# Splitting a single row maximum into two half products in a gated mix of two attentions

## The chip, the cores and the metric

The kernel runs on one core of one Trainium2 chip. The metric is the device time of one execution in microseconds; for the kernel before it was measured in three runs. Engines are named as in the profile: PE is TensorE's matmul, PEld its weight load, DVE is VectorE, ACT is ScalarE, POOL is GpSimd and SP is the queue that issues most DMAs.

## What is computed

The input x has 2048 rows of 512. Two attentions with 32 heads of 16 columns each are computed on it, and a gate per row mixes them. Branch A looks back at 8 keys in steps of two rows. Branch B lets all 32 query heads share one key head and one value head, over all 2048 keys. Everything is float32. The change touches branch B only.

```python
def _B_ref(x, wq, wk, wv, wo):
    q = (x @ wq).reshape(B, S, H, Dh).transpose(0, 2, 1, 3)
    k = x @ wk
    v = x @ wv
    scores = jnp.einsum("bhqd,bkd->bhqk", q, k) * (Dh ** -0.5)
    p = _softmax(scores, axis=-1)
    o = jnp.einsum("bhqk,bkd->bhqd", p, v)
    return o.transpose(0, 2, 1, 3).reshape(B, S, H * Dh) @ wo
...
x = A_x
g = _sigmoid((x * gate_w).sum(-1, keepdims=True))
return g * _A_ref(x, A_wqkv, A_wo) + (1 - g) * _B_ref(x, B_wq, B_wk, B_wv, B_wo)
```

## The kernel before

**Stages.** A front part (up to about 280 us) projects keys, values and queries. Then follows a loop of 512 steps plus one, in which branch B's attention runs on PE, ACT and DVE, while POOL works through branch A and DMAs move data between the two. Two output phases interrupt the loop; they multiply finished rows by the output weights. The last rows' output products are spread over the loop's last steps.

**Units and steps.** A unit is four heads and 512 queries; there are 32 units (`NU`). A step takes 128 keys for one unit, so a unit has 16 steps. The scores of a step are computed with keys on the partitions and queries along the free axis. `exp_pair` (line 570, its products at line 576) makes the *first scores*, two heads into the pair of banks pe0, and later in the step the *second scores*, the other two heads into pe1. Of the two heads, one uses array rows 0 to 63 and the other rows 64 to 127 (`odd`), so their two products can run side by side. Behind each, ACT takes one exponential of both banks (128x1024, line 578) into a tile `pexp`. Each bank pair exists once: the next step's first scores can be loaded only when the exponential that reads pe0 has ended, and so with pe1. At the end of a step `weighted` (line 586) multiplies the *previous* step's four `pexp` halves by the values, into the bank po; these products use all 128 rows of the array.

**Maxima ahead.** The exponentials need each query's largest score. It is computed for a later unit while the present one is in its steps, from products of its own: 128 queries against 512 keys, one head at a time (`max_mm`, line 395). A *pair* (`fill_pair`, line 425) computes both heads into the two banks of `pm` and VectorE reduces them in one instruction (line 433). A *single* (`fill_one`, line 437) computes one head into the bank `ps` (called `m1` in the code), which VectorE reduces at line 445. The results go to the unit's tile `mx`, one column per chunk of 512 keys; when all are there, `filled` reduces the columns (line 413), and a few small operations put the maxima into the query tile of the unit as extra rows. In output phases, sums and differences of keys (line 483) yield the maxima of two chunks at once.

**What sets the order.** The program is written out by a planner as it runs: `clk` holds its estimate of each engine's time, `free` when a bank will be free, and `T_...` its prices. A step's order is `(0, "m2", "later")`: first scores, a pair if its banks will be free, then the second scores with a single ahead of them or behind. `singles(s)` decides whether the step gets a single, from a running share and from how far DVE lags. `bare` remembers that the last step had none. The single goes ahead of the second scores if their banks are not expected to be free yet:

```python
if which == "later":
    order[:0] = ["m1", 1] if free["e1"] > clk["pe"] - E1S or bare[0] and free["m1"] < clk["pe"] - 1.0 else [1, "m1"]
    first = 0
```

A step without a single is called *plain* here, one with a single a *single step*. In the order of this kernel 209 steps are plain and 269 have a single, of which 60 have it behind the second scores; 34 further steps hold output products or end the loop. Plain and single steps mostly alternate. Every engine works through its instructions in the order of the program.

Of the kernel before, what the change touches and what calls it, by code (L numbers as in the profile page):

```python
# [6 lines left out]
F32 = mybir.dt.float32  # L7
F32R = mybir.dt.float32r
AF = mybir.ActivationFunctionType
ALU = mybir.AluOpType  # L10
AX = mybir.AxisListType
PSUM = bass.MemoryType.PSUM

P = 128
# [3 lines left out]
DH = 16  # L18
# [6 lines left out]
NU = NQB * NHG  # L25
# [10 lines left out]
NB = 10  # L36
# [14 lines left out]
LAG = 6  # L51


T_F, T_R, T_LAT, T_EXP, T_RED2, T_RED1, T_W, T_TTR = 0.235, 0.23, 0.20, 0.92, 1.14, 0.61, 1.21, 0.70


# [32 lines left out]
def gated_mix_kernel(ctx, tc, xt, wa, wk, wq, wo_a, wo_b, out):  # L89
    nc = tc.nc  # L90
# [42 lines left out]
    def after(eng, ready, dur):  # L133
        clk[eng] = max(clk[eng], ready) + dur
        return clk[eng]
# [91 lines left out]
    nc.vector.tensor_reduce(mk[:, 5:6], ident.rearrange("p (y s t) -> p y s t", s=2, t=8)[:, :, 1, :], AX.XY, ALU.add)  # L227
    nc.vector.tensor_scalar(mk[:, 4:5], mk[:, 5:6], -2.0, 1.0, op0=ALU.mult, op1=ALU.add)
    nc.vector.memset(mk[:, 6:7], -FMAX)
    whole_k = cp.tile([P, 2, DH], F32, name="wholek")  # L230
    halves_of = cp.tile([P, 2, P], F32R, name="sel")
    nc.vector.tensor_add(whole_k, twin[:, :, 0, :, 0], twin[:, :, 0, :, 1])
    for x in range(2):
# [139 lines left out]
    slots = [(0, 0, t, 2 * g + kc) for g in range(2) for t in range(2) for kc in range(2)]  # L373
    slots += [(0, pr, t, kc) for pr in range(2) for t in range(4) for kc in range(4) if pr or t > 1]
    slots += [(v, pr, t, kc) for v in range(1, NU) for pr in range(2) for t in range(4) for kc in range(4)]
    half = []
    free = {"m2": 0.0, "m1": 0.0, "e0": 0.0, "e1": 0.0, "po": 0.0}
    tasks, shifted = [], set()
    hooks, pool, done = [], 0.0, set()
# [1 line left out]
    def fillable():  # L381
        return bool(half) or bool(slots) and slots[0][0] < len(stacked) and stacked[slots[0][0]] <= clk["pe"]

    def unit_tile(v):
        for x in (v, v + 1):
            if x < NU and x not in left:
                mx[x] = wp.tile([P, 2, 2, 4, 4], F32, name="mx", bufs=3)
                nc.gpsimd.memset(mx[x], -FMAX)
                charge(250)
                left[x] = NF // NU  # L390
        return mx[v]
# [11 lines left out]
        issued[0] += 1  # L403

    def to_go():
        return 2 * len(slots) + len(half)

    def filled(v, n):
        left[v] -= n
        if not left[v]:  # L410
            ms = wp.tile([P, 2, 2, 8], F32, name="ms")
            m = mx.pop(v).rearrange("p b i t k -> p b (i t) k")
            nc.vector.tensor_reduce(ms, m.unsqueeze(2).to_broadcast([P, 2, 2, 8, 4]), AX.X, ALU.max)
            after("dve", 0, 0.32)
            if pe:
                tasks.append((clk["pe"] + 0.5, maxima_turn, (v, ms)))
            else:
                maxima_turn(v, ms)
# [3 lines left out]
        nc.vector.transpose(mt, ms.rearrange("p b x y -> p (b x y)"))  # L422
        tasks.append((after("dve", 0, 0.34) + (2.0 if formed and not pe else 0.1), shift_a, (v, mt)))

    def fill_pair(dst, key):
        if dst is m2:
            dst = m2.whole()
        v, pr, t, kc = slots.pop(0)
        m = unit_tile(v)
        mark("m20", "m21")  # L430
        for odd in range(2):
            max_mm(dst[:, odd, :], v, pr, t, kc, odd)
        nc.vector.tensor_reduce(m[:, :, pr, t, kc], dst, AX.X, ALU.max)  # L433
        free[key] = after("dve", after("pe", 0, T_R) + T_LAT, T_RED2) + 0.08
        filled(v, 2)

    def fill_one(dst=m1, key="m1"):
        if not half:
            v, pr, t, kc = slots.pop(0)
            half.extend([(v, pr, t, kc, 0), (v, pr, t, kc, 1)])  # L440
        v, pr, t, kc, odd = half.pop(0)
        m = unit_tile(v)
        mark(key)
        max_mm(dst, v, pr, t, kc, odd)
        nc.vector.tensor_reduce(m[:, odd, pr, t, kc:kc + 1], dst, AX.X, ALU.max)  # L445
        free[key] = after("dve", after("pe", 0, T_R) + T_LAT, T_RED1) + 0.08
        filled(v, 1)


    dd, formed, ended, wants = [], {}, set(), []  # L450
# [477 lines left out]
    def spread(js, n):  # L928

        m = 3 * (C + n)  # L930

        parts_a(js[0])
        yield 1.0
        while slots or half or free["m2"] > clk["pe"] + 0.1:
            yield 1.0
        for j in js:
            nxt = j + 1 if j != js[-1] else None
            items = []
            for i in range(m):
                if j == js[0] and i < 3 * C and (j, 1) not in turned:  # L940
                    while i == 3 * C - 3 and NU - 3 not in shaped:
                        yield 1.0
                    if NU - 3 in shaped:
                        prepare(j, n, nc.gpsimd.tensor_copy)
                items = items or out_items(j, n, (0, 1))
                st, mv = items[i]
                for b in range(2):
                    h = slice(64 * b, 64 * b + 64)
                    nc.tensor.matmul(m2[:, b, :], st()[h], mv[h], start=(i == 0), stop=(i == m - 1 and (b == 1 or nxt is not None)))  # L949
                after("pe", 0, T_R)  # L950
                row_prods[0] -= 1
                row_left[0] = m - 1 - i
                if i == 1 and j + 2 <= js[-1]:
                    blocks_both(j + 2)
                if i == 3 * C and nxt:
                    parts_a(nxt)
                if i < m - 1:
                    yield 0.0
            del turned[j, 0], turned[j, 1]
            if nxt:  # L960
                prepare(nxt, n, nc.gpsimd.tensor_copy)
            x = len(parts)
            if x < 2:
                spare.append((p2[0] if x else p2b[0]).tile([P, 512], F32, name="part", tag=("own", "tr8")[x], bufs=1))
            elif x == 2:
                two = p2[0].tile([P, 2, 512], F32, name="part", tag="pr", bufs=1)
                spare.extend([two[:, 0, :], two[:, 1, :]])
            parts[j] = spare[x]
            if nxt:
                nc.vector.tensor_copy(parts[j], m2[:, 1, :])  # L970
                nc.vector.tensor_add(parts[j], m2[:, 0, :], parts[j])
                after("dve", clk["pe"] + T_LAT, 1.4)
                yield 1.5
        done.add("last")
# [22 lines left out]
    def single_share(s):  # L997

        left = 16 * (NU - 1) - 16 - s
        if left > 0:  # L1000
            most = to_go() - 2 * left - PER_ROW * max(0, NJ - 4 - outs) - 2 * (left > 5)
            rate = most / left
            if len(stacked) < NU:
                ready = len(half) + 2 * sum(x[0] < len(stacked) for x in slots[:16 * NB])
                wait = max(1, 16 * (home(len(stacked))[1] + 1) + LAND - s)
                rate = min(rate, ready / wait - 2)
            share[0] = min(2.0, share[0] + max(0.0, min(1.0, rate)))
        else:
            share[0] = 1.0

    share, bare, step = [0.0], [False], [0]

    def fill_ready(key, slack):
        if fillable() and free[key] <= clk["pe"] + slack:
            clk["pe"] = max(clk["pe"], free[key])
            if key == "m1":
                fill_one()
            elif half and (not slots or slots[0][0] >= len(stacked) or stacked[slots[0][0]] > clk["pe"]):
                fill_one(m2[:, 0, :], "m2")
            elif slots:  # L1020
                fill_pair(m2, "m2")

    def pause(most):
        n = 0
        while n < most and slots and fillable():
            key = min(("e0", "e1", "m2"), key=lambda k: free[k])
            clk["pe"] = max(clk["pe"], free[key])
            if half:
                fill_one({"e0": eb[0], "e1": eb[1], "m2": m2}[key][:, 0, :], key)
                n += 1  # L1030
                continue
            fill_pair({"e0": eb[0], "e1": eb[1], "m2": m2}[key], key)
            n += 2
        return n
# [335 lines left out]
    for s in range(NS + 1):  # L1370
# [7 lines left out]
        if s < NS and kt == 0 and u not in shifted:  # L1378
            while u not in shifted:
                clk["pe"] += 0.5  # L1380
                run_tasks()
                if u not in shifted and left.get(u, 1):
                    assert pause(4)
        v = min(x[0][0] for x in (half, slots, [(NU,)]) if x)
        need = left.get(v, NF // NU)
        steps = 16 * v - 6 - s
        short = need - 2.8 * max(0, steps) if v < NU else 0
# [20 lines left out]
        elif short > 0 and steps < 2:  # L1408
            pause(short)

        first = 0
        some = min(4, -(-(row_prods[0] - TO_END) // (NS + 1 - s)))
        order = list(order)
        single_share(s)
        while order:
            which = order.pop(0)
            if which == "later":
                order[:0] = ["m1", 1] if free["e1"] > clk["pe"] - E1S or bare[0] and free["m1"] < clk["pe"] - 1.0 else [1, "m1"]
                first = 0
            elif which == "m2":  # L1420
                fill_ready("m2", M2S)
            elif which == "m1":
                one = not later_rows and (kt or not s or u >= NU - 8) and singles(s)
                bare[0] = not one
                if one:
                    first = half[0][4] if half else 0
                    fill_ready("m1", M1S)
            elif s < NS:
                if which == 1:
                    spread_some(some)  # L1430
                exp_pair(s, which % 2 or which // 2, which == 2, first)
# [9 lines left out]
    while later_rows:  # L1441
        clk["pe"] = max(clk["pe"], spread_at[0])
        spread_some(99)
        run_pool()
    assert not slots and not half and not hooks and not tasks and "last" in done, (len(slots), len(hooks), len(tasks), outs)


    tls, owns = [], []
# [73 lines left out]
```

## Time and profile before

| | |
|---|---|
| median of 3 runs | 1436.9 us (1436.71 to 1437.13) |
| profiled execution | 1437.89 us, span 1436.0 us |
| granted TensorE clock | 1.000 |
| PE busy | 1425.6 us (99% of the span) |
| ACT busy | 1298.0 us (90%) |
| DVE busy | 1141.4 us (79%) |
| POOL busy | 972.8 us (68%) |
| exponentials, line 578 | 1022, mean 1022 ns |
| pair reductions, line 433 | 482, mean 1224 ns |
| single reductions from ps, line 445 | 281, mean 680 ns |

A timeline row gives the start in the span, the length from the first instruction's start to the last one's end, engine, line, operation, out<-in, the shapes and how many instructions were merged; in brackets stands how long the engine was idle ahead of it and what ended that. An instruction's recorded start and end include its way through the pipeline, so consecutive products overlap in the records. In the page and the groups, a row ends with the idle time ahead of the group and what ended it.

### The profile page before, as it was taken

Reading aid. Unit: us, or ns where it says so; the run is one execution under the profiler, and the core shown is the slowest. Engines: PE = TensorE matmul, PEld = TensorE weight load, DVE = VectorE, ACT = ScalarE, POOL = GpSimd, SP = SyncE. Lnnn points to the kernel's source line nnn. Section 1 sums busy time; section 2 is a strip of 40 time slices with the busy share of each in tenths; the row PEclk is TensorE's granted clock in tenths of the full one; section 3 lists DMA queues with packets and bytes.
Section 4 is the critical chain, followed back from the end, with each engine's and each line's share of the span. In section 5 each row is a group of like instructions: output and inputs, shape, how many; then the busy total and the mean of one; then the engine's idle time right before and its main releaser. Section 6 shows DMA issues by size and latency. Waiting matters only on the chain.

```text
span 1436.0 us, 29352 instructions
## 1 busy us (share of the span) xinstructions
PE 1425.6 (99%) x10524; PEld 675.7 (47%) x10524; DVE 1141.4 (79%) x1887; ACT 1298.0 (90%) x1628; POOL 972.8 (68%) x1790
## 2 busy tenths in 40 slices
PE   9999999999999999999999999999999999999998
PEld 6877777633333333333333377333333337333343
DVE  8788889878877888888888788888888888888712
ACT  5899888899999999999999978999999997999986
POOL 6551688878889898988888988888888606011121
PEclk9999999999999999999999999999999999999999
DMA  7553533422112020012322211220211010000110
GB/s 244 155 151 103 150 106 106 121 55 88 43 57 88 13 77 31 32 65 43 97 70 63 73 35 54 79 62 31 72 43 43 17 36 25 9 2 2 27 35 30
DMA packets 107138, 94.37 MB, mean 66 GB/s; under 512 B 84964, under 2 KB 89100, under 8 KB 102896
## 3 DMA queue, kind: packets, MB, share of 16 engines
q1 hardware_dynamic: 100032, 53.30, 13.7%
q0 software_dynamic: 6240, 37.89, 7.9%
q8 instruction: 83, 1.36, 0.4%
q10 hardware_dynamic: 720, 1.31, 0.3%
q14 instruction: 63, 0.52, 0.1%
HBM read 62.13 MB, written 29.45 MB: 64 GB/s over the span
## 4 chain that ended last, share of the span: by engine, by line
PE 95%; DMA 1%; DVE 1%; POOL 1%; ACT 1%; issue 0%; SPq 0%; DVEq 0%; POOLq 0%; ACTq 0%
PE po L586 35%; PE pe L576 24%; PE pe L1215 11%; PE pm L395 8%; PE ps L395 4%; PE pe L895 4%; PE pm L483 3%; PE po L483 2%; PE ps L483 2%; PE pm L949 1%; DMA xraw<-xt 1%; DMA wqr<-wq 0%; DVE pexp L531 0%; POOL pr L650 0%; DVE osl L1478 0%
## 5 line engine op out<-in xcount | busy, mean ns | idle before, releaser
L578 ACT ACTIVATE pexp<-pe 128x1024 f32<-128x1024 f32 x1022 | 983.1, 1022 | 60.9 <-PE pe L576 58.4
L433 DVE TENSOR_REDUCE mx<-pm 128x2 f32<-128x1024 f32 x482 | 589.9, 1224 | 176.6 <-PE pm L395 174.1
L586 PE MATMUL po<-pexp,vst 128*32 128x512 f32 x4096 | 545.5, 605 | 0.4 <-DVE mx L531 0.4
L576 PE MATMUL pe<-qst,kst 64*128 64x512 f32 x1470 | 348.0, 455 | 1.5 <-ACT stage L330 0.8
L576 PEld LDWEIGHTS pe<-qst,kst 64*128 64x128 f32 x1470 | 138.4, 183 | 363.3 <-ACT pexp L578 356.2
L513 ACT ACTIVATE dd<-pm 128x512 f32<-128x512 f32 x292 | 168.6, 604 | 26.1 <-PE pm L483 7.5
L445 DVE TENSOR_REDUCE mx<-ps 128x1 f32<-128x512 f32 x281 | 191.0, 680 | 0.1
L650 POOL TENSOR_TENSOR pr<-aext 128x256 f32<-128x256 f32 x256 | 181.2, 736 | 4.7 <-DMA aext<-ad 4.5
L713 POOL TENSOR_TENSOR oa<-oa,av 128x256 f32<-128x256 f32 x224 | 164.5, 734 | 15.4
L710 POOL TENSOR_TENSOR av<-aext,lg 128x256 f32<-128x256 f32 x224 | 139.7, 624 | 13.0
L586 PEld LDWEIGHTS po<-pexp,vst 128*32 128x32 f32 x4096 | 80.5, 108 | 143.1 <-issue 133.9
L395 PE MATMUL pm<-kst,qst 62*128 62x512 f32 x677 | 136.0, 397 | 0.0
L1215 PE MATMUL pe<-wah,xh 64*128 64x512 f32 x384 | 128.7, 393 | 0.0
L1215 PE MATMUL pe<-wal,xh 64*128 64x512 f32 x384 | 128.7, 393 | 0.0
L1215 PE MATMUL pe<-wah,xl 64*128 64x512 f32 x384 | 128.5, 394 | 0.0
L531 DVE CUSTOM_DVE_ANT_0 dd<-po,dd 128x512 f32<-128x512 f32 x146 | 100.7, 690 | 18.4 <-PE po L483 7.1
L483 PE MATMUL pm<-kcd,qst 62*128 62x512 f32 x292 | 112.6, 397 | 0.0
L531 DVE CUSTOM_DVE_ANT_0 dd<-ps,dd 128x512 f32<-128x512 f32 x146 | 100.6, 689 | 13.4 <-PE ps L483 5.6
L613 POOL TENSOR_TENSOR rl<-rl,gate_t 128x16 f32<-128x16 f32 x31 | 6.9, 224 | 118.0 <-DVE rl L607 113.3
L656 POOL TENSOR_TENSOR tr<-pr 128x512 f32<-128x512 f32 x64 | 81.7, 1276 | 4.5
L395 PE MATMUL ps<-kst,qst 62*128 62x512 f32 x205 | 81.1, 396 | 0.9 <-DVE mx L445 0.9
L656 POOL TENSOR_TENSOR tr<-tr 128x256 f32<-128x256 f32 (+1 forms) x128 | 72.5, 567 | 9.0
(204 smaller groups left out, 2174.5 us busy)
## 6 DMA issues: line engine op xcount, KB each, us to landing
aext<-ad POOLq DMA_DIRECT2D x32, 1056.0 KB, 5.4
ad<-stage SPq DMA_DIRECT2D x32, 240.0 KB
qst<-qd SPq DMA_DIRECT2D x46, 128.0 KB
qd<-qhi SPq DMA_DIRECT2D x16, 256.0 KB
qd<-qlo SPq DMA_DIRECT2D x16, 256.0 KB
td<-raw SPq DMA_DIRECT2D x32, 128.0 KB
oa<-td SPq DMA_DIRECT2D x256, 16.0 KB
xraw<-xt SPq DMA_DIRECT2D x15, 256.0 KB
```

Source lines behind the costliest of these rows:

```text
L395: nc.tensor.matmul(dst, qst[home(v)[0]][b:b + 62, pr, t * P:(t + 1) * P], kst[b:b + 62, kc * 512:(kc + 1) * 512], start=True, stop=True)
L433: nc.vector.tensor_reduce(m[:, :, pr, t, kc], dst, AX.X, ALU.max)
L445: nc.vector.tensor_reduce(m[:, odd, pr, t, kc:kc + 1], dst, AX.X, ALU.max)
L483: nc.tensor.matmul(dst, qst[home(v)[0]][b:b + 62, pr, t * P:(t + 1) * P], kcd[b:b + 62, kc // 2, x, :], start=True, stop=True)
L513: nc.scalar.activation(d[:, odd], m2[:, odd, :], AF.Abs)
L531: nc.vector.tensor_tensor_reduce(d[:, odd], dst, d[:, odd], 1.0, -FMAX, ALU.add, ALU.max, m[:, odd, pr, t, kc:kc + 1])
L576: nc.tensor.matmul(bank[:, odd, :], kst[b:b + 64, kt * P:(kt + 1) * P], qst[home(u)[0]][b:b + 64, pr, :], start=True, stop=True)
L578: nc.scalar.activation(e, bank, AF.Exp, scale=SCALE)
L586: nc.tensor.matmul(po[32 * i:32 * i + 32, :], vst[:, kt, :], pexp[s, i // 2][:, i % 2, :], start=(kt == 0), stop=(kt == NJ - 1))
L650: nc.gpsimd.tensor_mul(pr[:, k], q, e[:, o:o + NH, AC:2 * AC])
L713: nc.gpsimd.tensor_add(ao, ao, av)
L1215: nc.tensor.matmul(front_bank(x), l[h], r[h], start=(not second and i == 0), stop=(second and i == 3 * C - 1))
```

## The change

Where a step follows one without a single, and the planner grants it a single, the single is now 256 keys of both heads in place of 512 keys of one head. Both results share the one bank `ps`: 256 columns for each head. The first head's product (`quarter_first`, array rows 0 to 63) stands behind the first scores and ahead of the pair; the second head's (`quarter_second`, rows 64 to 127) stands behind the second scores. The pair and the second scores of such a step start with the other half of the array (`first = 1`). Two products on different halves of the array that write one bank must not run at once, so VectorE gets an empty instruction that waits for the first product, and the second product waits for that. The reduction takes both heads at once (128x2x256). The tile `mx` gets eight columns in place of four, since a chunk of 512 keys can now arrive as two halves; its memset and its reduction become twice as wide. A half that is left over is computed alone into `pm` (`quarter_alone`). The grant is now decided ahead of the pair. The tile `wholek` moves to a rotating buffer.

```diff
+T_Q = 0.14
...
-    whole_k = cp.tile([P, 2, DH], F32, name="wholek")
+    whole_k = wp.tile([P, 2, DH], F32, name="wholek", tag="mt", bufs=2)
...
-                mx[x] = wp.tile([P, 2, 2, 4, 4], F32, name="mx", bufs=3)
+                mx[x] = wp.tile([P, 2, 2, 4, 8], F32, name="mx", bufs=3)
...
-            nc.vector.tensor_reduce(ms, m.unsqueeze(2).to_broadcast([P, 2, 2, 8, 4]), AX.X, ALU.max)
-            after("dve", 0, 0.32)
+            nc.vector.tensor_reduce(ms, m.unsqueeze(2).to_broadcast([P, 2, 2, 8, 8]), AX.X, ALU.max)
+            after("dve", 0, 0.45)
...
-        for odd in range(2):
+        for odd in (first, 1 - first):
             max_mm(dst[:, odd, :], v, pr, t, kc, odd)
...
+    def quarter_mm(dst, odd):
+        v, pr, t, kc, h = quarter[0]
+        b, k = 64 * odd, kc * 512 + h * 256
+        return nc.tensor.matmul(dst, qst[home(v)[0]][b:b + 62, pr, t * P:(t + 1) * P], kst[b:b + 62, k:k + 256], start=True, stop=True)
+
+    def quarter_max(src, key):
+
+        v, pr, t, kc, h = quarter.pop(0)
+        nc.vector.tensor_reduce(unit_tile(v)[:, :, pr, t, kc + 4 * h], src, AX.X, ALU.max)
...
+    def quarter_first():
+        if not quarter:
+            v, pr, t, kc = slots.pop(0)
+            quarter.extend((v, pr, t, kc, h) for h in range(2))
+        unit_tile(quarter[0][0])
+        mark("m1")
+        begun[0] = quarter_mm(m1[:, 0:256], 0)
+        after("pe", 0, T_Q)
+        begun[1] = nc.vector.nop()
+        after_that(begun[1], begun[0])
+
+    def quarter_second():
+        after_that(quarter_mm(m1[:, 256:512], 1), begun[1])
+        quarter_max(m1.rearrange("p (b k) -> p b k", b=2), "m1")
...
-            if which == "later":
+            if which == "m2" and s and order[0] == "later" and bare[0]:
+                one = not later_rows and (kt or u >= NU - 8) and singles(s)
+                split_max = one and free["m1"] <= clk["pe"] + 0.1 and (quarter or slots and slots[0][0] < len(stacked) and stacked[slots[0][0]] <= clk["pe"])
+                if split_max:
+                    quarter_first()
+                    first = 1
+                    order[:] = [1, "q"]
+                    bare[0] = False
+            if which == "q":
+                quarter_second()
+            elif which == "later":
...
-                fill_ready("m2", M2S)
+                fill_ready("m2", M2S, first)
```

The places below are the first steps of one unit, the one whose queries lie in qst_81. The first shows TensorE's order there before: pe_3943 is the bank pair of the first scores (pe0), pe_3991 that of the second (pe1), pm the pair's banks and ps the single's; a plain step is followed by a single step.

```order
L586 MATMUL po<-pexp,vst 32x512 x4
L576 MATMUL pe_3943<-qst_81,kst 128x512 x2
L395 MATMUL pm<-kst,ahead 128x512 x2
L576 MATMUL pe_3991<-qst_81,kst 128x512 x2
L586 MATMUL po<-pexp,vst 32x512 x4
L576 MATMUL pe_3943<-qst_81,kst 128x512 x2
L395 MATMUL pm<-kst,ahead 128x512 x2
L395 MATMUL ps<-kst,ahead 128x512
L576 MATMUL pe_3991<-qst_81,kst 128x512 x2
L586 MATMUL po<-pexp,vst 32x512 x4
```

In the changed kernel the first scores go to pe_3942 and the second to pe_3988; lines 619, 400, 629 and 458 are the scores, the pair, the weighted products and the half products:

```order
L629 MATMUL po<-pexp,vst 32x512 x4
L619 MATMUL pe_3942<-qst_81,kst 128x512 x2
L400 MATMUL pm<-kst,ahead 128x512 x2
L619 MATMUL pe_3988<-qst_81,kst 128x512 x2
L629 MATMUL po<-pexp,vst 32x512 x4
L619 MATMUL pe_3942<-qst_81,kst 128x512 x2
L458 MATMUL ps<-kst,ahead 128x256
L400 MATMUL pm<-kst,ahead 128x512 x2
L619 MATMUL pe_3988<-qst_81,kst 128x512 x2
L458 MATMUL ps<-kst,ahead 128x256
L629 MATMUL po<-pexp,vst 32x512 x4
```

The single's one product of 512 columns between the pair and the second scores is gone; one of 256 columns stands ahead of the pair and one behind the second scores. VectorE's order where a unit begins, before (tt is the copy of the finished unit's result, rl its reciprocal):

```order
L433 TENSOR_REDUCE mx<-pm 128x2
L600 STREAM_TRANSPOSE tt<-po 128x512
L433 TENSOR_REDUCE mx<-pm 128x2
L445 TENSOR_REDUCE mx<-ps 128x1
L607 RECIPROCAL rl<-tt 128x16
L433 TENSOR_REDUCE mx<-pm 128x2 x2
```

And in the changed kernel:

```order
L438 TENSOR_REDUCE mx<-pm 128x2
L643 STREAM_TRANSPOSE tt<-po 128x512
L438 TENSOR_REDUCE mx<-pm 128x2
L463 TENSOR_REDUCE mx<-ps 128x2
L650 RECIPROCAL rl<-tt 128x16
L438 TENSOR_REDUCE mx<-pm 128x2 x2
```

The reductions keep their places; the single's now yields two columns. The empty instruction, which the list doesn't show, stands ahead of the pair's reduction in every step with a split single.

In the whole loop 213 steps carry a split single and 44 a whole one (42 of them behind the second scores), and 221 are plain. All but one of the 213 follow a plain step. The second output phase comes at step 432, where it came at 416.

More of the change, by code (lines that the diff above doesn't have):

```diff
@@ L375, in gated_mix_kernel, with after_that @@
     slots += [(v, pr, t, kc) for v in range(1, NU) for pr in range(2) for t in range(4) for kc in range(4)]
-    half = []
+    half, quarter, begun = [], [], [None, None]
+    def after_that(x, y):
+        tc.add_manual_dep(x.ins, y.ins.name, mybir.DependencyInfo(mybir.DependencyClass.Sync, mybir.DependencyReason.DATA), reason="bank")
     free = {"m2": 0.0, "m1": 0.0, "e0": 0.0, "e1": 0.0, "po": 0.0}
@@ L405, in to_go @@
     def to_go():
-        return 2 * len(slots) + len(half)
+        return 2 * len(slots) + len(half) + len(quarter)
     def filled(v, n):
@@ L447, in fill_one, with quarter_alone @@
         filled(v, 1)
+    def quarter_mm(dst, odd):
[5 more added lines that the diff above has]
+        nc.vector.tensor_reduce(unit_tile(v)[:, :, pr, t, kc + 4 * h], src, AX.X, ALU.max)
+        free[key] = after("dve", clk["pe"] + T_LAT, T_RED1) + 0.08
+        filled(v, 1)
+    def quarter_first():
[11 more added lines that the diff above has]
+        quarter_max(m1.rearrange("p (b k) -> p b k", b=2), "m1")
+    def quarter_alone():
+        dst = m2.whole()
+        clk["pe"] = max(clk["pe"], free["m2"])
+        mark("m20", "m21")
+        for odd in range(2):
+            quarter_mm(dst[:, odd, 0:256], odd)
+        after("pe", 0, T_R)
+        quarter_max(dst[:, :, 0:256], "m2")
     dd, formed, ended, wants = [], {}, set(), []
@@ L933, in spread @@
         yield 1.0
-        while slots or half or free["m2"] > clk["pe"] + 0.1:
+        while slots or half or quarter or free["m2"] > clk["pe"] + 0.1:
             yield 1.0
@@ L1003, in single_share @@
             if len(stacked) < NU:
-                ready = len(half) + 2 * sum(x[0] < len(stacked) for x in slots[:16 * NB])
+                ready = len(half) + len(quarter) + 2 * sum(x[0] < len(stacked) for x in slots[:16 * NB])
                 wait = max(1, 16 * (home(len(stacked))[1] + 1) + LAND - s)
@@ L1011, in gated_mix_kernel, with fill_ready @@
     share, bare, step = [0.0], [False], [0]
-    def fill_ready(key, slack):
-        if fillable() and free[key] <= clk["pe"] + slack:
+    def fill_ready(key, slack, first=0):
+        if key == "m2" and quarter and not half and not (slots and slots[0][0] < len(stacked)) and free[key] <= clk["pe"] + slack:
+            quarter_alone()
+        elif fillable() and free[key] <= clk["pe"] + slack:
             clk["pe"] = max(clk["pe"], free[key])
@@ L1020, in fill_ready @@
             elif slots:
-                fill_pair(m2, "m2")
+                fill_pair(m2, "m2", first)
     def pause(most):
         n = 0
+        if quarter:
+            quarter_alone()
+            n += 1
         while n < most and slots and fillable():
@@ L1383, in gated_mix_kernel @@
                     assert pause(4)
-        v = min(x[0][0] for x in (half, slots, [(NU,)]) if x)
+        v = min(x[0][0] for x in (half, quarter, slots, [(NU,)]) if x)
         need = left.get(v, NF // NU)
@@ L1409, in gated_mix_kernel @@
             pause(short)
-        first = 0
+        first, one, split_max = 0, None, False
         some = min(4, -(-(row_prods[0] - TO_END) // (NS + 1 - s)))
@@ L1420, in gated_mix_kernel @@
             elif which == "m2":
-                fill_ready("m2", M2S)
+                fill_ready("m2", M2S, first)
             elif which == "m1":
-                one = not later_rows and (kt or not s or u >= NU - 8) and singles(s)
+                if one is None:
+                    one = not later_rows and (kt or not s or u >= NU - 8) and singles(s)
                 bare[0] = not one
@@ L1444, in gated_mix_kernel @@
         run_pool()
-    assert not slots and not half and not hooks and not tasks and "last" in done, (len(slots), len(hooks), len(tasks), outs)
+    assert not slots and not half and not quarter and not hooks and not tasks and "last" in done, (len(slots), len(hooks), len(tasks), outs)
     tls, owns = [], []
```

2 lines of the change are left out of this document (1 added, 1 removed).

## The prediction

> **What bounds the kernel now.** I read the page first, then the waits, then the timeline of a few steps engine by engine. The page's rows for busy time and for the chain that ended last:
>
> ```profile
> PE 1425.6 (99%) x10524; PEld 675.7 (47%) x10524; DVE 1141.4 (79%) x1887; ACT 1298.0 (90%) x1628; POOL 972.8 (68%) x1790
> PE 95%; DMA 1%; DVE 1%; POOL 1%; ACT 1%; issue 0%; SPq 0%; DVEq 0%; POOLq 0%; ACTq 0%
> L578 ACT ACTIVATE pexp<-pe 128x1024 f32<-128x1024 f32 x1022 | 983.1, 1022 | 60.9 <-PE pe L576 58.4
> ```
>
> TensorE is busy 99% of the span, and ScalarE 90%. That alone says: take products off TensorE. But matmul records are pipelined, and a busy PE row need not be a PE that streams. The longest entry of the list of waits is a weight load that waits for ScalarE:
>
> ```profile
> PEld pe L576 <- ACT pexp L578: 497.0, 916, 1.2
> ```
>
> So I look at one plain step (702.34 to 704.23) and the single step behind it (704.23 to 706.36). First PE's rows, then its weight loads, then ScalarE:
>
> ```profile
> 702.34 0.50 PE L576 MATMUL pe<-qst,kst 64*128 64x512 f32 x2
> 702.68 0.40 PE L395 MATMUL pm<-kst,qst 62*128 62x512 f32 x2
> 702.91 0.39 PE L576 MATMUL pe<-qst,kst 64*128 64x512 f32 x2
> 703.24 1.06 PE L586 MATMUL po<-pexp,vst 128*32 128x512 f32 x8
> 704.23 0.50 PE L576 MATMUL pe<-qst,kst 64*128 64x512 f32 x2
> 704.57 0.39 PE L395 MATMUL pm<-kst,qst 62*128 62x512 f32 x2
> 704.80 0.39 PE L395 MATMUL ps<-kst,qst 62*128 62x512 f32 x1
> 704.94 0.49 PE L576 MATMUL pe<-qst,kst 64*128 64x512 f32 x2
> 705.36 1.07 PE L586 MATMUL po<-pexp,vst 128*32 128x512 f32 x8
> 706.36 0.50 PE L576 MATMUL pe<-qst,kst 64*128 64x512 f32 x2
> ```
>
> ```profile
> 704.40 0.19 PEld L395 LDWEIGHTS pm<-kst,qst 62*128 62x128 f32 x2
> 704.58 0.19 PEld L395 LDWEIGHTS ps<-kst,qst 62*128 62x128 f32 x1
> 704.93 0.19 PEld L576 LDWEIGHTS pe<-qst,kst 64*128 64x128 f32 x2 [0.17 <-ACT pexp L578]
> ```
>
> ```profile
> 702.94 3.83 ACT L578 ACTIVATE pexp<-pe 128x1024 f32<-128x1024 f32 x4 [0.21 <-PE pe L576]
> 706.96 1.94 ACT L578 ACTIVATE pexp<-pe 128x1024 f32<-128x1024 f32 x2 [0.18 <-PE pe L576]
> ```
>
> The plain step takes 1.89 us, the single step 2.13, together 4.02. In the single step the second scores start only at 704.94. Their weight load came at 704.93, and it waited for ScalarE, not for the single. The time of that load can be worked out from the step ahead. The plain step starts at 702.34. Its first exponential starts at 702.94, 0.60 later. It had waited 0.21 us for these very scores. The two exponentials of a step take 1.94 us from the first's start to the second's end (706.96 row), so the second ends at 704.88, and that is the one that reads the bank which the next step's second scores overwrite. The load follows 0.05 later: 0.60 + 1.94 + 0.05 = 2.59 after the start of the plain step. Nothing that TensorE does in the single step can bring it forward. The single at 704.80 lies in a gap that would be there without it.
>
> Two places show that gap bare. Late in the kernel a plain step stands behind a plain step, and at 421.00 a step has a single and no pair:
>
> ```profile
> 1349.43 0.50 PE L576 MATMUL pe<-qst,kst 64*128 64x512 f32 x2
> ...
> 1351.34 0.50 PE L576 MATMUL pe<-qst,kst 64*128 64x512 f32 x2
> 1351.68 0.40 PE L395 MATMUL pm<-kst,qst 62*128 62x512 f32 x2
> 1352.04 0.50 PE L576 MATMUL pe<-qst,kst 64*128 64x512 f32 x2
> 1352.47 1.06 PE L586 MATMUL po<-pexp,vst 128*32 128x512 f32 x8
> 1353.46 0.50 PE L576 MATMUL pe<-qst,kst 64*128 64x512 f32 x2
> ```
>
> ```profile
> 1352.03 0.19 PEld L576 LDWEIGHTS pe<-qst,kst 64*128 64x128 f32 x2 [0.36 <-ACT pexp L578]
> ```
>
> ```profile
> 421.00 0.50 PE L576 MATMUL pe<-qst,kst 64*128 64x512 f32 x2
> 421.35 0.39 PE L395 MATMUL ps<-kst,ahead 62*128 62x512 f32 x1
> 421.70 0.50 PE L576 MATMUL pe<-qst,kst 64*128 64x512 f32 x2
> ...
> 423.13 0.50 PE L576 MATMUL pe<-qst,kst 64*128 64x512 f32 x2
> ```
>
> The step from 1351.34 has no single and takes 2.12 us all the same; the load at 1352.03 comes 2.60 after 1349.43. The step from 421.00 has two products fewer than a full single step and takes 2.13. So behind a plain step a step lasts 2.59 + 0.44 (load of the second scores to the weighted products, 1352.03 to 1352.47) + 0.99 (1352.47 to 1353.46) = 4.02 after the plain step began, and a whole single ahead of the second scores is free there.
>
> **The change part by part.** In the order of the changed kernel 213 steps carry a split maximum, and 212 of them stand behind a plain step. Each takes the whole single out of the free gap. Its first half goes ahead of the pair, into the same gap, so it costs nothing. Its second half goes behind the second scores, and there nothing is free. Both heads' second scores leave the same wait together, so both halves of the array end together, and the weighted products (128 rows) need both. What a product costs behind the second scores is shown by the steps of the old kernel that put a whole single there; one such step, and the plain step behind it:
>
> ```profile
> 1285.39 0.40 PE L576 MATMUL pe<-qst,kst 64*128 64x512 f32 x2
> 1285.63 0.39 PE L395 MATMUL ps<-kst,qst 62*128 62x512 f32 x1
> 1285.95 1.06 PE L586 MATMUL po<-pexp,vst 128*32 128x512 f32 x8
> ...
> 1287.52 0.40 PE L576 MATMUL pe<-qst,kst 64*128 64x512 f32 x2
> 1287.86 1.06 PE L586 MATMUL po<-pexp,vst 128*32 128x512 f32 x8
> ```
>
> From the second scores to the weighted products it is 0.56 us with the product and 0.34 without: 0.22. The two step lengths above give 2.13 - 1.89 = 0.24. I take 0.23 for a whole product. The trace has no product of 256 columns. Its price lies between 0.07 (half of the shortest distance of two starts above, 704.80 to 704.94) and 0.23 (as much as 512 columns); I take half of 0.23, 0.115, because both products stream their columns at the same width. The terms:
>
> - 213 second halves x 0.115 = +24.5 us.
> - The order has 257 steps with a single or a split one in place of 269, and 221 plain ones in place of 209 (the rest of the maxima goes to the output phases). 12 x 0.23 = -2.8.
> - Plain steps that stand behind plain steps, and so gain nothing, are 6 in place of 2: 4 x 0.23 = +0.9.
> - The two output phases take 16 more products on one half of the array. Two products side by side take 0.23 (702.68 to 702.91), one 0.115: +1.8.
>
> Sum: +24.4. The profiled execution took 1437.89 (its span of 1436.0 and 1.9 around it), 1.0 over the median of the runs shown (1436.9). So 1462.3 for such an execution, and 1461.3 for the median. By the Trainium skill, "TensorE: Matmul & The Clock Gate", section "Back-to-back issue gap", a product of 256 columns takes 262 cycles and one of 512 takes 518, 0.109 and 0.216 us at its 2.4 GHz; as an estimate the first term would be 23.2 us by it. No row here shows 256 columns; for 512 the rows above have 0.22 to 0.24.
>
> The edits that I cost at nothing, each with its cover:
>
> - The second half waits for an empty instruction on VectorE, and that for the first half. VectorE's rows for the two steps:
>
> ```profile
> 703.12 1.23 DVE L433 TENSOR_REDUCE mx<-pm 128x2 f32<-128x1024 f32 x1 [0.16 <-PE pm L395]
> 705.01 1.23 DVE L433 TENSOR_REDUCE mx<-pm 128x2 f32<-128x1024 f32 x1 [0.66 <-PE pm L395]
> ```
>
> VectorE is through with the last step's pair at 704.35 and idle until 705.01. A 512-column product that starts at 704.57 (pm) releases it 0.44 later; one of half the columns some 0.11 sooner, 0.33 after its start. From VectorE's end to the load on PE it is 0.05 (704.35 to 704.40). The first half would start at 704.57, so PE has its answer near 704.95 plus the empty instruction's own time. The second half is due only behind the second scores, whose loads come at 704.93 and which fill 0.23. Cover: 0.2 us. Queued behind the empty instruction is the pair's reduction, which needs a later product anyway; behind the second half on PE stand the weighted products. If the answer is later than that, each tenth costs 213 x 0.1 = 21 us.
> - The pair's second product starts behind the first half, some 0.115 later. It is still over before 704.94. Its weights can load meanwhile: the load for ps at 704.58 starts while both products of pm run. The reduction of the pair ends 0.12 later in the step, but the next pair's product is a step away.
> - The maxima's tile is twice as wide. Its rows in the groups are these:
>
> ```profile
> L413 DVE TENSOR_REDUCE ms<-mx 128x32 f32<-128x128 f32 x32 | 9.2, 287 | 1.1
> L388 POOL MEMSET mx<- 128x64 f32 x32 | 5.0, 160 | 0.0
> ```
>
> Doubled, they would add 9.2 us to VectorE, which idles 0.66 us in each such step, and 5.0 to GpSimd, which is busy 68%. Neither is on the path.
> - The second output phase comes a unit later (step 432 in place of 416), with its copies, stores and row loads. The queues hold the same instructions, and what waits for the phase is only the end of the kernel. The tile "wholek" moves into a rotating buffer long before its first other user.
>
> **The rivals.** *The split pays.* If TensorE were bound by its products, as 99% and the chain's 95% suggest, each split would give the idle half of the array something to do: 0.115 less in 213 steps, -24.5, and with the other terms (-0.1) 1412.3. The double rows speak for it: two products of a pair stand as one 0.40 us entry, hardly longer than one alone. The Trainium skill says the same in "TensorEngine Tiling (Array Packing)", section "Key Properties": different tiles load weights and multiply in parallel, so an idle half is waste; the trace agrees that they overlap. Against it stand the loads at 704.93 and 1352.03, which wait for ScalarE, and 4.02 us that don't shrink when the single is absent. It decides if the second scores' load in split steps comes 0.1 us sooner than 2.59 after the plain step's start. 6 in 100.
>
> *The second half hides.* If the weighted products' own start (0.34 behind the second scores, 0.23 of it streaming) had room for 0.115, the first term is gone: -0.1, 1436.8 for the median. The step with the whole product (0.56) speaks against it: nothing of that product was hidden. 7 in 100.
>
> *The answer comes late.* If the empty instruction's way through VectorE takes 0.3 us and not 0.1, the second half starts 0.1 later, and the weighted products with it: 213 x 0.215 = 45.8, minus 0.1, 1482.6. The trace has no such instruction, so the cover of 0.2 is all that speaks against it. 7 in 100.
>
> **How the numbers follow.** The forecast, 1461.3, has 80 in 100. Its price bounds give 213 x 0.07 = 14.9 and 213 x 0.23 = 49.0, with -0.1: 1451.7 and 1485.8. The range 1450 to 1486 holds nearly all of the forecast and the late answer, and leaves out the first two rivals (13 in 100) and a little beyond the bounds. The measurement of this kernel can tell 0.2%, 2.9 us. Faster by more: 0.06. Within it: 0.07. Slower by more: 0.87.
>
> **What would show it.** Right: in split steps the second scores' load still comes about 2.59 after the plain step's start with a wait for "ACT pexp" of more than 0.3 us, as at 1352.03; the second half starts about 0.34 behind it (704.23 to 704.57 is that distance for products behind a load just made); the weighted products start some 0.2 after the second half (0.32 at 1285.63, less 0.115); a split step lasts about 2.25 us, plain ones still 1.89, the pair 4.14; ScalarE's idle time behind "PE pe" grows. Wrong: a split step of 2.02 us (the first rival), of 2.13 (the second), or of 2.35 with a wait for VectorE ahead of the second half (the third). If split steps last 2.25 and the whole doesn't move by 24 us, the other steps have changed, and my counts miss something.

## The result, and the profile after

The changed kernel takes 1461.21 us (median of 4 runs, 1460.89 to 1462.21), the kernel before 1437.02 (4 runs). The ratio is 1.0166, 95% interval 1.0154 to 1.0179: 24.2 us slower, where the prediction had 24.4. The profiled execution took 1461.1 us with a span of 1459.0, 23.0 over the span before.

The page's rows for busy time, the chain and the exponentials, then the entry of the waits that was quoted before:

```profile
PE 1446.3 (99%) x10738; PEld 698.2 (48%) x10738; DVE 1143.9 (78%) x1893; ACT 1304.0 (89%) x1640; POOL 972.9 (67%) x1790
PE 93%; DVE 2%; ACT 1%; POOL 1%; DMA 1%; SPq 1%; issue 1%; DVEq 0%; ACTq 0%; POOLq 0%
L621 ACT ACTIVATE pexp<-pe 128x1024 f32<-128x1024 f32 x1022 | 983.2, 1022 | 81.2 <-PE pe L619 78.1
```

```profile
PEld pe L619 <- ACT pexp L621: 466.6, 750, 0.9
```

PE is as busy as before (99%), and there lies the lesson: the busy share can't tell a full step from a step that waits between products whose records overlap. What shows the loss is ScalarE's idle time behind PE, 78.1 us in place of 58.4, with the same 1022 exponentials of the same length. A plain step and the split step behind it, in PE's, PEld's, ScalarE's and VectorE's rows:

```profile
712.26 0.50 PE L619 MATMUL pe<-qst,kst 64*128 64x512 f32 x2
...
714.17 0.51 PE L619 MATMUL pe<-qst,kst 64*128 64x512 f32 x2
714.50 0.28 PE L458 MATMUL ps<-kst,qst 62*128 62x256 f32 x1
714.51 0.50 PE L400 MATMUL pm<-kst,qst 62*128 62x512 f32 x2
714.86 0.50 PE L619 MATMUL pe<-qst,kst 64*128 64x512 f32 x2
715.20 0.28 PE L458 MATMUL ps<-kst,qst 62*128 62x256 f32 x1
715.40 1.06 PE L629 MATMUL po<-pexp,vst 128*32 128x512 f32 x8
716.40 0.50 PE L619 MATMUL pe<-qst,kst 64*128 64x512 f32 x2
```

```profile
714.86 0.19 PEld L619 LDWEIGHTS pe<-qst,kst 64*128 64x128 f32 x2 [0.17 <-ACT pexp L621]
714.97 0.19 PEld L458 LDWEIGHTS ps<-kst,qst 62*128 62x128 f32 x1
```

```profile
712.87 3.84 ACT L621 ACTIVATE pexp<-pe 128x1024 f32<-128x1024 f32 x4 [0.30 <-PE pe L619]
```

```profile
715.05 1.23 DVE L438 TENSOR_REDUCE mx<-pm 128x2 f32<-128x1024 f32 x1 [0.78 <-PE pm L400]
```

The second scores' load comes at 714.86, 2.60 us after the plain step began, as before. The second half starts 0.34 behind it and the weighted products 0.20 behind that. The plain step takes 1.91 us, the split step 2.23, the pair 4.14 in place of 4.02. ScalarE waits 0.30 at the plain step's first exponential, where it waited 0.21.

### The profile page after: what moved, and what is told of

Same layout as the page of the kernel before. It is cut to its first block, busy times and chain, and to the rows that moved or that the text cites. A ratio compares the mean times of both kernels' runs of the same rounds, so it can differ in the third digit from the quotient of the medians.

```text
span 1459.0 us, 30009 instructions
## 1 busy us (share of the span) xinstructions
PE 1446.3 (99%) x10738; PEld 698.2 (48%) x10738; DVE 1143.9 (78%) x1893; ACT 1304.0 (89%) x1640; POOL 972.9 (67%) x1790
## 4 chain that ended last, share of the span: by engine, by line
PE 93%; DVE 2%; ACT 1%; POOL 1%; DMA 1%; SPq 1%; issue 1%; DVEq 0%; ACTq 0%; POOLq 0%
PE po L629 33%; PE pe L619 24%; PE pe L1263 11%; PE pm L400 8%; PE pe L938 4%; PE pm L526 3%; PE ps L458 3%; PE po L526 2%; PE ps L526 2%; PE pm L992 1%; PE ps L400 1%; PE pe L254 1%; DMA td<-raw 1%; ACT pexp L621 1%; DVE mx L438 0%
## 5 line engine op out<-in xcount | busy, mean ns | idle before, releaser
L621 ACT ACTIVATE pexp<-pe 128x1024 f32<-128x1024 f32 x1022 | 983.2, 1022 | 81.2 <-PE pe L619 78.1
L438 DVE TENSOR_REDUCE mx<-pm 128x2 f32<-128x1024 f32 x476 | 582.8, 1224 | 193.8 <-PE pm L400 191.3
L400 PE MATMUL pm<-kst,qst 62*128 62x512 f32 x672 | 149.3, 396 | 2.0 <-DVE mx L438 1.8
L463 DVE TENSOR_REDUCE mx<-ps 128x2 f32<-128x512 f32 x213 | 145.4, 683 | 1.8 <-PE ps L458 1.8
L526 PE MATMUL pm<-kcd,qst 62*128 62x512 f32 x302 | 118.4, 397 | 0.0
L400 PEld LDWEIGHTS pm<-kst,qst 62*128 62x128 f32 x672 | 87.2, 186 | 5.0 <-DVE mx L438 3.8
L556 ACT ACTIVATE pexp<-pm 128x512 f32<-128x512 f32 x120 | 67.6, 599 | 17.4 <-PE pm L526 10.2
L458 PE MATMUL ps<-kst,qst 62*128 62x256 f32 x290 | 80.6, 278 | 0.0
```

Source lines behind the costliest of these rows:

```text
L400: nc.tensor.matmul(dst, qst[home(v)[0]][b:b + 62, pr, t * P:(t + 1) * P], kst[b:b + 62, kc * 512:(kc + 1) * 512], start=True, stop=True)
L463: nc.vector.tensor_reduce(unit_tile(v)[:, :, pr, t, kc + 4 * h], src, AX.X, ALU.max)
L526: nc.tensor.matmul(dst, qst[home(v)[0]][b:b + 62, pr, t * P:(t + 1) * P], kcd[b:b + 62, kc // 2, x, :], start=True, stop=True)
L556: nc.scalar.activation(d[:, odd], m2[:, odd, :], AF.Abs)
L621: nc.scalar.activation(e, bank, AF.Exp, scale=SCALE)
```

## Experiments

The theory: ScalarE's two exponentials of a plain step hold the second scores of the next step until 2.59 us after the plain step's start. What stands ahead of the second scores there is free; what stands behind them is paid by its columns. The rivals: TensorE is bound by the sum of its products wherever they stand; or the way through VectorE and back costs; or the split itself does.

### Without the singles ahead of the second scores

The kernel before, with those products left out:

```diff
-        max_mm(dst, v, pr, t, kc, odd)
+        if product:
+            max_mm(dst, v, pr, t, kc, odd)
...
-                fill_one()
+                fill_one(product=not (1 in order))
```

> The kernel before without the 208 single products that stand ahead of the second scores (206 in full single steps); VectorE still reduces the bank in their place, so it finds old numbers, and those maxima are wrong. The 60 singles behind the second scores stay. Theory (the singles ahead of the second scores lie in a gap that ScalarE holds open): nothing is gained, single steps still last 2.11 to 2.13, the time 1433 to 1437. Rival (TensorE is bound by its products): the steps without them last 1.90, 206 x 0.235 less, 1389.

Measured: 1433.96 us, ratio 0.9971 (0.9960 to 0.9982), 4 us for 208 products. Two steps on PE, both without a single:

```profile
702.09 0.50 PE L577 MATMUL pe<-qst,kst 64*128 64x512 f32 x2
702.43 0.40 PE L395 MATMUL pm<-kst,qst 62*128 62x512 f32 x2
702.67 0.42 PE L577 MATMUL pe<-qst,kst 64*128 64x512 f32 x2
703.02 1.06 PE L587 MATMUL po<-pexp,vst 128*32 128x512 f32 x8
704.01 0.50 PE L577 MATMUL pe<-qst,kst 64*128 64x512 f32 x2
...
704.68 0.50 PE L577 MATMUL pe<-qst,kst 64*128 64x512 f32 x2
705.11 1.06 PE L587 MATMUL po<-pexp,vst 128*32 128x512 f32 x8
706.11 0.49 PE L577 MATMUL pe<-qst,kst 64*128 64x512 f32 x2
```

```profile
704.68 0.19 PEld L577 LDWEIGHTS pe<-qst,kst 64*128 64x128 f32 x2 [0.34 <-ACT pexp L579]
```

The pair of steps takes 4.02 us, to the hundredth what it took with a single in it. The load at 704.68 comes 2.59 after 702.09. The single steps don't all keep the 2.11 to 2.13 of the expectation: two neighbouring steps now share the 4.02 us in varying parts. Here they last 1.92 and 2.10, a few steps further on 1.98 and 2.04; of the 415 steps without a single 121 last under 1.95 us and 116 over 2.10. The pair of steps keeps its length (median 4.02). The rival's 1389 is excluded.

### Whole singles behind the second scores

The kernel before, with one line changed:

```diff
-                order[:0] = ["m1", 1] if free["e1"] > clk["pe"] - E1S or bare[0] and free["m1"] < clk["pe"] - 1.0 else [1, "m1"]
+                order[:0] = [1, "m1"]
```

> The kernel before, with every whole single of 512 keys behind the second scores, also in the some 206 steps that had it ahead of them. Theory (behind a plain step ScalarE holds the second scores until 2.59 us after the plain step began, and a product behind them is paid in full, by its columns): these steps last 2.13 + 0.22 to 0.24 = 2.36, and the time is 1437 + 206 x 0.23 = 1484. Rival (TensorE is bound by its products wherever they stand): no change, 1437, since the products are the same.

Measured: 1480.75 us, ratio 1.0297 (1.0281 to 1.0312). The step behind a plain step:

```profile
714.11 0.49 PE L576 MATMUL pe<-ahead,kst 64*128 64x512 f32 x2
...
714.75 0.50 PE L576 MATMUL pe<-ahead,kst 64*128 64x512 f32 x2
715.10 0.40 PE L395 MATMUL ps<-kst,qst 62*128 62x512 f32 x1
715.42 1.06 PE L586 MATMUL po<-pexp,vst 128*32 128x512 f32 x8
716.42 0.50 PE L576 MATMUL pe<-ahead,kst 64*128 64x512 f32 x2
```

The same products in another place cost 43 us, where 47 were expected, and ScalarE's idle time behind PE grows by as much, from 58.4 to 101.9 us. The 205 steps with a single behind a plain step have a mean of 2.352 us, 0.22 over 2.13; the split steps of the changed kernel have a median of 2.238, 0.108 over a median of 2.130. The 63 steps whose single does not follow a plain step last 2.13, as before. From the product to the weighted products it is 0.32 us here and 0.20 with half the columns. So half the columns cost half.

### The first half alone

The changed kernel without the second half's product:

```diff
-        after_that(quarter_mm(m1[:, 256:512], 1), begun[1])
         quarter_max(m1.rearrange("p (b k) -> p b k", b=2), "m1")
```

> The changed kernel without the second half's product: the split step computes only the first head's 256 keys, and the reduction finds old numbers in the second half of the bank, so the maxima are incomplete. Everything else, the empty instruction on VectorE among it, stays. Theory (the first half lies in the gap ahead of the second scores and is free, the second half costs all of it): split steps back to 2.13 us, the time back to about 1437 (213 x 0.11 less than 1461). Rival (the two products share the cost, or the disturbed pair does: its second product starts late): a split step between 2.13 and 2.25, about 1449 if half of it is the first product's.

Measured: 1441.68 us, ratio 1.0024 (1.0014 to 1.0035). Of the 24 us 20 go with the second half. The split steps are down to a median of 2.115, below the single steps of 2.13, so the first half costs nothing there. The 4 us that remain are elsewhere: the plain steps have a mean of 1.931 us where the changed kernel has 1.902 and the kernel before 1.911. In one of them VectorE is late for the pair: its reductions follow each other with no wait, and the pair's load comes 0.24 into the step (701.87 to 702.11), where the kernel before has 0.11 (706.36 to 706.47). PEld's and VectorE's rows of the first half alone, then PEld's row of the kernel before:

```profile
701.87 0.19 PEld L618 LDWEIGHTS pe<-qst,kst 64*128 64x128 f32 x2 [0.84 <-ACT pexp L620]
702.11 0.19 PEld L400 LDWEIGHTS pm<-kst,qst 62*128 62x128 f32 x2
```

```profile
700.86 1.19 DVE L438 TENSOR_REDUCE mx<-pm 128x2 f32<-128x1024 f32 x1
701.97 0.68 DVE L463 TENSOR_REDUCE mx<-ps 128x2 f32<-128x512 f32 x1
```

```profile
706.47 0.19 PEld L395 LDWEIGHTS pm<-kst,qst 62*128 62x128 f32 x2
```

Against the kernel before, the plain steps are 4.4 us longer in all and the output phases 3.2 (both together, with the step behind each); the split steps are 5.2 us shorter than as many single steps. That the plain steps' part is VectorE's in all of them is likely and was not taken apart.

### Both halves for one head, without the way through VectorE

The changed kernel, with 256 keys and then 256 more of the same head, so on the same half of the array, and no wait between them:

```diff
-        b, k = 64 * odd, kc * 512 + h * 256
+        b, k = 64 * h, kc * 512 + odd * 256
...
-        begun[1] = nc.vector.nop()
-        after_that(begun[1], begun[0])
...
-        after_that(quarter_mm(m1[:, 256:512], 1), begun[1])
-        quarter_max(m1.rearrange("p (b k) -> p b k", b=2), "m1")
+        quarter_mm(m1[:, 256:512], 1)
+        quarter_max(m1, "m1")
```

> The split maximum with both halves for one head: 256 keys behind the first scores, the other 256 keys of the same head behind the second scores, on the same half of the array, so no empty instruction on VectorE and no wait for it; the order is the changed kernel's otherwise. Theory (the place of the second half costs, not the wait): 1461 again, within 2 us, split steps 2.24. Rival (the way through VectorE and back costs): faster than 1461 by what the wait cost, down to 1437 if it was all of it.

Measured: 1462.68 us, ratio 1.0172 (1.0157 to 1.0187), the same as the change itself. So the wait for VectorE costs nothing where the change puts it. The changed kernel's own trace says why: the empty instruction appears on VectorE's sequencer with 21 ns, and it starts 0.66 us into the split step (median), while the second half's load comes at 0.80, right behind the second scores' loads at 0.70.

```profile
L475 DVEq EVENT_SEMAPHORE  x213: 21/21/21, 284.0 to 1366.6; - x107
```

### The second half ahead of the second scores

```diff
-                    order[:] = [1, "q"]
+                    order[:] = ["q", 1]
```

> The changed kernel with the second half ahead of the second scores instead of behind them (behind the pair). Theory: the wait for VectorE's answer now matters. The answer is there 0.66 us after the step's start in the profile of the changed kernel, so the second half can load at about 0.72 and the second scores, behind it in order, stream about 0.1 later than ScalarE allows: split steps of 2.20 to 2.25, 1451 to 1461. Rival (only the place behind the second scores is dear, and the answer comes early enough): 2.13, 1437.

Measured: 1468.2 us, ratio 1.0210 (1.0195 to 1.0226): worse than the change, and 7 us beyond what the theory had. Here the wait for VectorE does bind:

```profile
713.83 0.18 PEld L458 LDWEIGHTS ps<-kst,qst 62*128 62x128 f32 x1 [0.20 <-DVEq L475]
713.83 0.29 PEld L619 LDWEIGHTS pe<-qst,kst 64*128 64x128 f32 x2
```

The step began at 713.10. The second half loads at 0.73, not the 0.72 that I had as the least, and both second scores stand behind it in PE's order: they end 0.14 later than in a single step, so the step lasts 2.27 us. The gap is open for a product that needs no answer, such as the whole single; a round trip through VectorE uses it up. I had let only one of the two second scores wait.

### Nothing that holds the second scores

Both kernels without the second exponential of every step (the weighted products use the first one's tile for all four heads):

```diff
-        e = px.tile([P, 2, 512], F32, name="pexp", bufs=6)
-        nc.scalar.activation(e, bank, AF.Exp, scale=SCALE)
+        e = pexp[s, 0] if pr else px.tile([P, 2, 512], F32, name="pexp", bufs=6)
+        if not pr:
+            nc.scalar.activation(e, bank, AF.Exp, scale=SCALE)
```

The kernel before:

> The kernel before without the second exponential of every step: the second scores are computed, but nothing reads them, and the weighted products use the first exponential's tile for all four heads. The order of all other instructions is kept. It takes away what holds the second scores. Theory: the single steps don't get shorter, since the single fills the time the gap leaves (first scores, pair, single, second scores, weighted products: 2.13), plain steps 1.89: 1435 to 1437. Rival (ScalarE itself sets the pace): clearly faster, under 1420.

Measured: 1432.64 us, 2.4 under the least that the theory had, and far from the rival's 1420. The single steps keep a mean of 2.136 us (2.139 with all exponentials) and the plain ones have 1.894 (1.911). So two limits lie side by side in the kernel before: the order of TensorE's products alone takes 1.89 + 2.13 = 4.02 us for two steps, and the chain through ScalarE takes 4.02 with no single in it. Taking away one of the two gains 4 or 5 us.

The changed kernel:

> The changed kernel without the second exponential of every step, as in the run beside it. Theory: with nothing that holds the second scores, the idle half of the array is worth what the change meant: a split step lasts 2.02 (1.90 + 0.115), 213 x 0.11 less than a single step of 2.13, so this kernel is faster than the kernel before without its second exponentials: about 1412 against 1436, the sign of the change turned round. Rival (a product behind the second scores always costs, or the split itself does): slower than the run beside it by about 24 us, as 1461 against 1437.

Measured: 1423.58 us, 9 us faster than the run beside it; against the whole kernel before on the same chip the ratios are 0.9900 (0.9887 to 0.9914) and 0.9962 (0.9949 to 0.9976). The sign is turned round, as the theory said. A split step without the wait:

```profile
702.77 0.50 PE L619 MATMUL pe<-qst,kst 64*128 64x512 f32 x2
703.12 0.28 PE L458 MATMUL ps<-kst,qst 62*128 62x256 f32 x1
703.12 0.51 PE L400 MATMUL pm<-kst,qst 62*128 62x512 f32 x2
703.35 0.52 PE L619 MATMUL pe<-qst,kst 64*128 64x512 f32 x2
703.59 0.31 PE L458 MATMUL ps<-kst,qst 62*128 62x256 f32 x1
703.83 1.06 PE L630 MATMUL po<-pexp,vst 128*32 128x512 f32 x8
704.82 0.50 PE L619 MATMUL pe<-qst,kst 64*128 64x512 f32 x2
```

It lasts 2.05 us (median 2.038), where the single steps of the run beside it keep 2.13. The size was missed: 9 us in place of 24. By the median, 213 x 0.098 (2.136 less 2.038) = 21 come from the split steps, and 2 from fewer single steps. Some 8.5 are given back in 17 late split steps, in most of which PE waits for VectorE to free the pair's banks, 3 in the output phases and the front, and 3 in plain and whole single steps. The longest of the late steps, in PE's rows and VectorE's row:

```profile
912.73 0.50 PE L619 MATMUL pe<-qst,kst 64*128 64x512 f32 x2
913.07 0.28 PE L458 MATMUL ps<-kst,qst 62*128 62x256 f32 x1
915.26 0.50 PE L400 MATMUL pm<-kst,qst 62*128 62x512 f32 x2 [1.91 <-DVE mx L438]
```

```profile
913.65 0.45 DVE L831 STREAM_TRANSPOSE raw<-oa 128x256 f32<-128x256 f32 x1 [2.14 <-POOL oa L757]
```

VectorE is not busy there. The next instruction in its order is a transposing copy of branch A's result (raw<-oa), which waits 2.14 us for GpSimd, and the reduction that frees the pair's banks stands behind it (914.02 to 915.21).

### The split behind steps that had a single

The change moved to where the theory has nothing that holds the second scores:

```diff
-            if which == "m2" and s and order[0] == "later" and bare[0]:
+            if which == "m2" and s and order[0] == "later" and not bare[0]:
...
-                split_max = one and free["m1"] <= clk["pe"] + 0.1 and (...)
+                split_max = one and free["m1"] <= clk["pe"] + 0.3 and (...)
```

> The split maximum where it should pay: behind a step that had a single, in place of a whole single behind the second scores; behind a plain step the whole single stays ahead of the second scores. In the order 30 steps carry a split one, 225 a whole one (7 of them behind the second scores, 60 before) and 223 none. Theory (behind a single step ScalarE has let go of the bank by 0.46 us, and nothing is held): a split step lasts 2.02 in place of 2.13. 223 x 1.90 + 225 x 2.135 + 30 x 2.02 = 964.7 against 209 x 1.90 + 269 x 2.135 = 971.4 before: 6.7 less in the steps, some 2 more in the output phases, which take the 17 singles' work: about 1432. Rival (a split step costs more than a whole single wherever it stands, 2.25): 1439.

Measured: 1449.8 us, ratio 1.0082 (1.0069 to 1.0096). This missed: the split steps last 2.33 us, not 2.02. The reason is a wait that neither side had:

```profile
1029.29 0.19 PEld L619 LDWEIGHTS pe<-qst,kst 64*128 64x128 f32 x2 [0.84 <-ACT pexp L621]
1029.83 0.18 PEld L458 LDWEIGHTS ps<-kst,qst 62*128 62x128 f32 x1 [0.35 <-DVE mx L450]
1029.83 0.29 PEld L400 LDWEIGHTS pm<-kst,qst 62*128 62x128 f32 x2
```

```profile
1029.09 0.68 DVE L450 TENSOR_REDUCE mx<-ps 128x1 f32<-128x512 f32 x1
```

The bank ps is still being reduced from the step ahead, until 1029.77; the first half loads 0.06 later, 0.54 into the step, and the pair and the second scores stand behind it. That explains 30 x 0.3 = 9 of the 18 us between 1432 and 1449.8. The output phases are 3.7 us longer than before, and one step with a whole single waited 1.5 us; what remains of the difference was not taken apart. With one bank for singles, a step behind a single step has no room for a first half ahead of its pair. No version here that computes everything beats the kernel before.

## Why the prediction was right

*What bounds the step.* It rested on one sum: 0.60 + 1.94 + 0.05 = 2.59 us from a plain step's start to the next step's second scores. The trace after has 2.60 (712.26 to 714.86). The run without the singles shows the reading of the kernel before to be right: 208 products could be left out of a PE that reads 99% busy, for 4 us, because they lay in that gap. The 4.02 us that two steps last without them are the chain through ScalarE: 2.59 to the second scores' load, 0.43 to the weighted products, 1.00 to the next step (702.09, 704.68, 705.11, 706.11).

*The price of the second half.* The prediction had 0.115, half of a whole product. One of the two figures behind it, the 0.24 from the lengths of two steps, was not a price by its own argument, since ScalarE's hold sets the length of that single step; that the lengths stay without the hold, in the run without second exponentials, showed only later that 0.24 is about what the product costs there. Taken from the starts of the first scores in both traces, the 213 split steps sum to 479.1 us, 23.6 over as many single steps at the old mean of 2.138; the forecast was 24.5. The median step pays 0.108, 23.0 in all; late steps, of which the kernel before has some too, make up the rest. The longest, at 938.43, lasts 3.71 us; in PE's rows and VectorE's row:

```profile
938.43 0.50 PE L619 MATMUL pe<-qst,kst 64*128 64x512 f32 x2
938.76 0.28 PE L458 MATMUL ps<-kst,qst 62*128 62x256 f32 x1
940.37 0.50 PE L400 MATMUL pm<-kst,qst 62*128 62x512 f32 x2 [1.32 <-DVE mx L438]
```

```profile
938.75 0.45 DVE L830 STREAM_TRANSPOSE raw<-oa 128x256 f32<-128x256 f32 x1 [1.76 <-POOL oa L756]
```

There PE waits for the pair's banks, of which the prediction said nothing: VectorE stands idle at a copy of branch A's result that waits for GpSimd, with the pair's reduction behind it (939.12 to 940.31). With a like step at 964.88, where the copy waits for a DMA, this costs 2.1 us. The estimate of 23.2 that was worked out from the Trainium skill's page "TensorE: Matmul & The Clock Gate", section "Back-to-back issue gap", lies as near: its 0.109 for 256 columns, which the page gives for an isolated product, stands against the 0.108.

*The small terms.* Twelve single steps fewer were forecast, -2.8. The trace after has 46 steps with a whole single, not 44, so ten fewer, -2.3 by the old means; these whole singles last 0.6 longer in all than at the old mean. The plain steps behind plain steps were put at +0.9; the plain steps as a whole came out 2.1 us under the old mean, so that term did not show. The output phases were put at +1.8 and took 2.9 (with the step behind each). Together 23.6 - 2.3 + 0.6 - 2.1 + 2.9 = 22.7 of the 23.0 us between the spans. That the small terms nearly cancel, as forecast, is in part luck, since each is off by 0.5 to 3.

*The cover of the wait.* The prediction had 0.2 us, with PE's answer near 0.72 into the step. The instruction starts at 0.66, and the run without it is as slow as the run with it. That held, with less to spare than 0.2: it is the second half's load that waits, the answer let it load at 0.73 in the run that put it ahead, and behind the second scores it comes at 0.80.

*What it got wrong.* It expected a wait of more than 0.3 us for "ACT pexp" at the second scores' load. The row has 0.17, since the pair's second weight load now ends later (its records run from 714.32 to 714.69), so PEld is idle for less; the load's time is what the argument needed, and that held. The first rival's premise, that an idle half of the array is waste, was sound: without the hold a split step is 0.09 shorter than a single step. It failed on the place, not on the array. The Trainium skill's "TensorEngine Tiling (Array Packing)", section "Key Properties", says that different tiles can load weights and multiply in parallel, and the rows of that run agree: the half product and the first product of the pair, on the other half of the array, both start at 703.12.

## What to carry to other kernels

A product is worth what its place is worth. Before halving or packing work on a busy engine, find the wait that ends last in the step, and see which side of it the work is on: ahead of the wait it was free already, and each part that moves behind it is paid in full. Two neighbouring steps of different content with the same length, or one step without the work and as long as the others, show such a gap in the profile when the busy share reads 99%. Where two limits lie side by side, as here TensorE's order and the chain through ScalarE, taking away one gains little: 4 or 5 us of 1437.

## What was not expected of the hardware

- Without the singles the lengths of neighbouring steps wandered, from 1.90 and 2.12 to 2.03 and 1.99 and back, where 1.90 and 2.13 had alternated; the pair kept 4.02. A length that belongs to two steps can't be read from one.
- An empty instruction for VectorE took 21 ns on its sequencer, and its way from the first half's start (0.34 into the step) to its own start (0.66) took 0.32 us.
- VectorE, busy 77 to 80% in all of these kernels, still set the length of some steps, up to 5.29 us (a split step of the changed kernel without second exponentials): not by being busy, but by standing idle at a copy that waited 2.14 us for GpSimd, with a pair's reduction behind it.
